# A prologue that takes its bound from the first parts of the keys, and more fill in the first turns: attention beside a long convolution on one Trainium2 core

## The chip, the core and the metric

The kernel runs on one core of one Trainium2 chip (trn2). The metric is the time of one execution on the device in microseconds (us); of several runs the median is taken. Besides the runs there is one profiled execution, whose trace is quoted here. Engines: PE multiplies matrices (PEld loads its weights), ACT applies functions, DVE and POOL work element by element, SP issues DMAs.

## The reference

Two independent parts, written side by side into the output: attention with 32 query heads of 16 columns and one shared key and value head over 2048 positions, and a gated long convolution of 512 channels.

```python
q = (x @ wq).reshape(B, S, 32, 16).transpose(0, 2, 1, 3)
k, v = x @ wk, x @ wv                                  # one head, 16 columns
p = softmax(einsum("bhqd,bkd->bhqk", q, k) * 16 ** -0.5)
a = einsum("bhqk,bkd->bhqd", p, v) -> (B, S, 512) @ wo
...
kv = short_conv(k2, shift_k) * v2                      # four taps
b = q2 * (irfft(rfft(kv, 2S) * rfft(ssm_k, 2S))[:S] + kv * ssm_D)
return concatenate([a, b], -1)                         # x: 1 x 2048 x 512
```

## The kernel before, in words

**The main loop.** Queries are cut into 32 stacks; a stack is four heads and 512 positions. For each stack there are 16 blocks of 128 keys in two halves, `a` = 0 and 1, which gives 1016 tiles on this path. A tile is eight products of PE (`keys`, L937: keys 32 x 49 rows against queries) into a two-bank tile `s`, one exponential of ACT over 128 x 1024 (`exp`, L949), and in a later turn the products of the exponentials with the values (`pv`, L973). There are two `s` tiles in PSUM (pool `ps`), so the scores of tile t wait for the exp of tile t - 2. Two further two-bank tiles (pool `pf`, `pair()`) serve everything else.

**Numbers in parts.** A float32 operand is written as a sum of two float16 parts, "first" (`hi`) and "second" or lower (`lo`), and a product is taken as first x first + lower weight x first + first x lower. A row of a stack holds 49 entries: first part of q (rows 0 to 15), its lower part (16 to 31), a bound of the scores (row 32), and the first part again (33 to 48). The bound keeps the exponentials in range; it is made from the largest |k| and from |q| (`first_bound`, `first_rows`; `bound` for the later stacks). The largest |k| comes from `k_max`.

**The prologue** (`prologue`, before tile 0). x comes in four chunks of 512 positions, each as two DMAs on SP's queue. A chunk is turned by PE (`x_turn`, L576), ACT writes the first part (L589) and DVE the lower (L592). Stack 0's queries are made from chunk 0 (L770, twelve products), cut (L683), sent to DRAM as parts (`q_send`), and read back as a stack (`stack`, L893). k and v are one product of 32 columns (`kv`, L601, 48 products over four chunks), copied by ACT (L611); its rows are spread over the partitions by a float32 product (`kv_rows`, L617), clipped (`k_cut`, L622) and combined (`k_rows`, L629) into the key tile `kst`, chunk by chunk of 512 keys; the first 256 keys go ahead. `v_turn` (L635, L638) turns v. Products on zeros (`warm`, L567) stand between.

**Behind the prologue.** `attend` walks over the tiles. Each turn emits the scores and exp of tile x + 2, the value products that its plan gives, and then "fill" from eight threads (the rest of the queries, the convolution, the output projection, a spill of turned chunks to DRAM). `_Fill.turn` decides how much: it keeps a running lateness of PE in ns (a turn is `SLOT` = 916, scores 220, a value product pair 430, a fill product 216) and lets fill in as long as it stays below `LATE` = 200. `yield WAIT, n` is a thread's request to be left alone for 2n turns. `rest_of_q` makes key chunks 2 and 3 in its first turns, then the bound of the first group, then the other queries. The order of instructions on each engine is exactly the order in which they are written (a manual schedule), and an engine that waits holds up all behind it.

Of the kernel before, what the change touches and what calls it, by code (L numbers as in the profile page):

```python
# [8 lines left out]
F32 = mybir.dt.float32  # L9
F32R = mybir.dt.float32r  # L10
BF16 = mybir.dt.bfloat16
# [8 lines left out]
P = 128  # L20
# [29 lines left out]
SLOT, SCORES, PV, UNIT, LATE = 916, 220, 430, 216, 200  # L50
# [59 lines left out]
class _Emit:  # L110
# [421 lines left out]
    def load(self):  # L532
# [6 lines left out]
        nc.scalar.dma_start(wkv[:, :, DH:32], I["A_wv"].rearrange("(k p) e -> p k e", p=P))  # L539
        self.msk = self.c.tile([P, 295], F32, name="msk")  # L540
        nc.scalar.dma_start(self.msk, I["msk"])
        xa = w.tile([P, 4, D], F32, tag="sp", bufs=1, name="xa")
# [12 lines left out]
        for g in range(1, 4):  # L555
            nc.sync.dma_start(wqf[g], wq[:, :, g * P : (g + 1) * P])
# [4 lines left out]
        self.parts(nc.gpsimd, self.wkv[:, 0], self.wkv[:, 1], wkv, WS)  # L561
        self.wqf = wqf
# [6 lines left out]
    def x_turn(self, c, b, between=lambda: None, cut=None):  # L569

        nc = self.nc

        def turn(dp, rows):
            for e in range(2):
                for i in rows:
                    nc.tensor.transpose(  # L576
                        b[dp][:, e, i * P : (i + 1) * P],
                        self.xin[c][i // 2][:, i % 2, (2 * dp + e) * P : (2 * dp + e + 1) * P],
                        self.ident,
                    )  # L580

        for rows in (range(2), range(2, 4)):
            for dp in range(2):
                turn(dp, rows)
            if rows.start == 0:
                between()
        for dp in range(2):
            hi, lo = (self.xT[c][:, i, 2 * dp : 2 * dp + 2, :] for i in range(2))
            nc.scalar.mul(hi, b[dp], XS)  # L589
            if cut is not None and dp == 0:  # L590
                self.q_hi(0, 0, cut)
            nc.vector.scalar_tensor_tensor(lo, b[dp], XS, hi, ALU.mult, ALU.subtract)  # L592
        if cut is not None:
            self.q_abs(0, 0, cut)

    def kv(self, b):

        order = [(i, j, dk) for dp in range(2) for i, j in ((0, 0), (1, 0), (0, 1)) for dk in (2 * dp, 2 * dp + 1)]
        for x in order:
            for c in range(4):  # L600
                self.nc.tensor.matmul(  # L601
                    b[32 * c : 32 * c + 32, :],
                    self.wkv[:, x[0], x[2], :],
# [27 lines left out]
    def v_turn(self, kv, b):  # L631

        nc = self.nc
        for t in range(4):
            nc.tensor.transpose(b[:, t * P : (t + 1) * P], kv[:, t * P : (t + 1) * P], self.ident)  # L635
# [831 lines left out]
```

## Time and profile before

| | us |
|---|---|
| runs, median of 3 | 1006.04 (1002.65 to 1006.18) |
| profiled execution | 1004.97 |
| its span, first to last instruction | 1003.1 |
| PE, ACT, DVE, POOL busy | 941.7, 951.4, 744.6, 172.7 |
| mean granted TensorE clock | 0.992 of full |

A row of a timeline has the start in us, the length, the engine, the line of the kernel, the operation, what it writes and reads, its shape and a count; in brackets the idle time before it and what ended that. Rows of groups have a count, then busy us and the mean in ns of one, then the idle time before them.

### The profile page before, as it was taken

The numbers are of one execution on the slowest core, as the hardware profiler recorded it, in microseconds if no ns is written. First come the engines' busy times: TensorE is split into PE (matmuls) and PEld (weight loads), VectorE is DVE, ScalarE is ACT, GpSimd is POOL, SyncE is SP. The second block draws the span as 40 slices with busy tenths as digits, with TensorE's granted clock in tenths as the row PEclk, the third lists the DMA queues.
The fourth block names the chain that finished last, engine by engine and source line by source line (L and its number), as shares of the span: only waits on it lengthen the run. The fifth ranks groups of instructions, "written<-read, shape, count | busy, mean of one in ns | idle before, by whom it ended". The sixth has DMA issues, their size and how long they took to land.

```text
span 1003.1 us, 51275 instructions
## 1 busy us (share of the span) xinstructions
PE 941.7 (94%) x23471; PEld 459.7 (46%) x23471; DVE 744.6 (74%) x963; ACT 951.4 (95%) x1033; POOL 172.7 (17%) x305
## 2 busy tenths in 40 slices
PE   7999999999999999999989999999889989989996
PEld 4344454444544444444544545444334444444453
DVE  4637966988528988989888688599998828667752
ACT  4699999999999999989999999999999999999994
POOL 2442211410004000100054353000000032111000
PEclk9799999999999999999999999999999999999999
DMA  6262442333213111222143344111111143121101
GB/s 228 82 191 77 134 125 86 106 91 91 71 55 99 62 44 45 87 85 65 44 141 120 95 148 125 43 42 37 54 44 44 48 124 109 55 71 43 49 10 47
DMA packets 69461, 83.12 MB, mean 83 GB/s; under 512 B 20816, under 2 KB 58550, under 8 KB 69238
## 3 DMA queue, kind: packets, MB, share of 16 engines
q1 hardware_dynamic: 47430, 43.78, 13.7%
q0 software_dynamic: 20320, 35.46, 12.1%
q8 instruction: 185, 3.03, 1.3%
q10 hardware_dynamic: 1488, 0.54, 0.2%
q14 instruction: 38, 0.31, 0.1%
HBM read 54.66 MB, written 25.03 MB: 79 GB/s over the span
## 4 chain that ended last, share of the span: by engine, by line
PE 51%; ACT 25%; DVE 14%; issue 6%; DMA 2%; SPq 0%; POOL 0%; ACTq 0%; DVEq 0%
ACT p L949 25%; PE f L973 24%; PE s L937 14%; PE f L250 11%; DVE own L1036 3%; DVE sp L169 1%; DVE ao L982 1%; DMA xb<-in_A_x 1%; DVE sp L290 1%; DVE ao L983 1%; DMA qd<-qp 1%; DVE sp L435 0%; PE f L617 0%; DVE own L1025 0%; DVE t L435 0%
## 5 line engine op out<-in xcount | busy, mean ns | idle before, releaser
L949 ACT ACTIVATE p<-s 128x1024 f32<-128x1024 f32 x1016 | 938.3, 1067 | 18.4 <-PE s L937 16.3
L973 PE MATMUL f<-p,vx 64*32 64x512 f32 (+1 forms) x8880 | 551.1, 555 | 1.8 <-DVE cut L683 1.1
L937 PE MATMUL s<-st,kst 49*32 49x512 f16 x8128 | 427.7, 382 | 33.3 <-ACT p L949 29.2
L937 PEld LDWEIGHTS <-kst 49*32 49x32 f16 x8192 | 199.8, 89 | 400.0 <-issue 353.8
L973 PEld LDWEIGHTS f<-p,vx 64*32 64x32 f32 x8880 | 175.8, 106 | 30.1 <-issue 4.6
L169 DVE TENSOR_TENSOR sp<-sp 128x1024 f32<-128x1024 f32 x96 | 111.1, 1215 | 0.0
L290 DVE COPY sp<-f 128x1024 f32<-128x1024 f32 x32 | 39.1, 1223 | 64.9 <-PE f L250 64.8
L295 POOL DMA_DIRECT2D ff<-in_ff x64 | 34.7, 546 | 277.1 <-ACT p L949 275.6
L982 DVE COPY ao<-f 128x512 f32<-128x512 f32 (+1 forms) x33 | 22.2, 674 | 56.7 <-PE f L973 56.6
L250 PE MATMUL f<-wo,o 64*32 64x512 f16 x1440 | 57.1, 375 | 1.7 <-DVE cut L683 0.9
L169 DVE TENSOR_TENSOR sp<-sp,sp 128x1024 f32<-128x1024 f32 x48 | 56.1, 1217 | 0.3
L250 PE MATMUL f<-xT,wq 64*32 64x512 f16 x1344 | 52.8, 375 | 1.7 <-DVE gm L733 1.2
L295 POOL DMA_DIRECT2D fi<-in_fi x32 | 17.8, 562 | 180.4 <-ACT p L949 180.4
L250 PE MATMUL f<-hT,ff 64*32 64x256 f32 x1024 | 40.8, 377 | 1.3 <-DVE sp L290 1.2
L250 PE MATMUL f<-a,ff 64*32 64x256 f32 x1024 | 41.2, 378 | 0.7 <-DVE a L407 0.6
L467 DVE TENSOR_TENSOR r<-f,q 128x512 f32<-128x512 f32 x16 | 11.0, 689 | 41.2 <-PE f L250 41.2
L250 PE MATMUL f<-sp,fi 64*32 64x256 f32 x1024 | 40.3, 376 | 0.9 <-DVE r L467 0.9
L469 POOL DMA_DIRECT2D out<-r x32 | 17.8, 562 | 124.6 <-DVE r L467 114.0
L405 DVE TENSOR_TENSOR a<-a,t 128x512 f32<-128x512 f32 x48 | 33.2, 692 | 1.6
L396 DVE TENSOR_TENSOR t<-kk,tpb 128x512 f32<-128x512 f32 (+1 forms) x50 | 33.0, 663 | 0.8 <-DMA qd<-qp 0.8
L323 POOL DMA_DIRECT2D hin<-in_B_ssm_k x32 | 21.1, 663 | 64.4 <-ACT p L949 63.0
L250 PEld LDWEIGHTS <-o 64*32 64x32 f16 x1440 | 22.8, 93 | 15.6 <-DVE wp L1156 1.5
(166 smaller groups left out, 731.1 us busy)
## 6 DMA issues: line engine op xcount, KB each, us to landing
ff<-in_ff POOLq DMA_DIRECT2D x64, 128.0 KB, 2.9
od<-ao SPq DMA_DIRECT2D x60, 128.0 KB
qd<-qp SPq DMA_DIRECT2D x48, 128.0 KB
st<-qd SPq DMA_DIRECT2D x62, 98.0 KB
kk<-in_B_k POOLq DMA_DIRECT2D x32, 128.0 KB, 2.9
v<-in_B_v POOLq DMA_DIRECT2D x32, 128.0 KB, 3.2
hin<-in_B_ssm_k POOLq DMA_DIRECT2D x32, 128.0 KB, 5.5
fi<-in_fi POOLq DMA_DIRECT2D x32, 128.0 KB, 3.0
```

The costliest lines, as they stand in the source:

```text
L169: v.tensor_tensor(part(out), part(a), part(b), op)
L250: y = self.nc.tensor.matmul(out[j : j + 32, cols], w[r, j : j + 32], x[r], start=half == m == 0, stop=half == 1 and m == k - 1,)
L290: self.nc.vector.tensor_copy(out, self.both.rearrange("p i (q n) -> p i q n", q=2))
L295: self.paced(self.nc.gpsimd.dma_start(t[:, i], self.I[n][:, 2 * m2 + i]))
L323: self.paced(nc.gpsimd.dma_start(dst, src))
L396: nc.vector.tensor_tensor(out[:, n], kk[:, x], tap(i, n.stop - n.start), ALU.mult)
L405: nc.vector.tensor_tensor(a, a, t, ALU.add)
L937: self.nc.tensor.matmul(s[j : j + 32, e, :], self.kst[rows, k * P + j : k * P + j + 32], self.st[n][rows, a, cols], start=True, stop=True,)
L949: self.exps[u % 4] = self.nc.scalar.activation(self.pt[u], s, AF.Exp, scale=LN2 * DH**-0.5 / SC / SC)
L973: nc.tensor.matmul(self.acc[e][32 * j : 32 * j + 32, m], vx[rows, :], y, start=k == 0, stop=stop)
L982: nc.vector.tensor_copy(a, self.acc[0][:, m])
L1036: v.scalar_tensor_tensor(g, g if i < 4 else y, c[i], y if i else x.bitcast(BF16), ALU.add, ALU.mult)
```

## The change

It has five parts.

1. The bound of stack 0 is made from a largest |k| that `kv_max` computes from first parts alone (16 products of 32 columns, all four chunks, in their own bank). The first 256 keys are computed apart (`kv_first`, 12 products of 16 columns). The full k and v follow in three groups (`kv(.., 0, 0)`, `(1, 0)`, `(0, 1)`); for chunk 3 the third group moves into `rest_of_q`, and so do the other keys of chunks 2 and 3, v of chunk 3, and a second run of `k_max` over the final k, which checks that the first bound was large enough.
2. Chunk 3 is turned right behind chunk 2, without the query products between; ACT saves its turned values to `xa` and its lower part is made later (`rest_of_q`). The products on zeros between the steps are gone, except the first ten.
3. Stack 0's queries go from the on-chip parts straight into the stack tile by twelve copies on SP (`first_stack`); the copies to DRAM and the loads of the other groups' query weights come behind them. POOL makes the first part of the queries; it also makes the parts of v's weights between the query's two parts, and their load goes to the end of SP's x loads.
4. One of the two rows of the bound is written by ACT instead of DVE. Stack 2 is loaded at the 22nd tile of stack 1 instead of the 6th.
5. `LATE` becomes 290 for the first 288 turns and stays 200 afterwards.

```diff
-SLOT, SCORES, PV, UNIT, LATE = 916, 220, 430, 216, 200
+SLOT, SCORES, PV, UNIT = 916, 220, 430, 216
+LATE, FULL = (290, 200), 288
...
+    def kv_max(self, b, c, dks):
+        for dk in dks:
+            for i in c:
+                self.nc.tensor.matmul(
+                    b[32 * i : 32 * i + 32], self.wkv[:, 0, dk, :], self.xT[i][:, 0, dk, :], start=dk == 0, stop=dk == 3
+                )
...
     def first_rows(self, b, st, a):
-        for e in range(2):
-            r = slice(BR + 64 * e, BR + 64 * e + 1)
-            self.nc.vector.tensor_scalar(st[r, a, :], b[r, e, :], f, -60000.0, ALU.mult, ALU.max)
+        r = [slice(BR + 64 * e, BR + 64 * e + 1) for e in range(2)]
+        self.nc.vector.tensor_scalar(st[r[0], a, :], b[r[0], a, :], f, None, ALU.mult)
+        self.nc.scalar.activation(st[r[1], a, :], b[r[1], a, :], AF.Copy, scale=f)
+    def first_stack(self, qp):
+        t = self.w.tile([P, 2, 512], F16, tag="st", bufs=2, name=self.nm("st"))
+        for a in range(2):
+            for i, rows in ((0, (0, BR + 1)), (1, (DH,))):
+                for r in rows:
+                    for e in range(2):
+                        h = DH * (e + 2 * a)
+                        self.nc.sync.dma_start(t[64 * e + r : 64 * e + r + DH, a, :], qp[h : h + DH, i, :])
...
+        cut = self.q_cut(q)
+        nc.gpsimd.tensor_scalar(qp[:, 0, :], cut, 1.0, None, ALU.mult)
+        self.kv_parts(slice(DH, 32))
+        nc.gpsimd.tensor_tensor(qp[:, 1, :], cut, qp[:, 0, :], ALU.subtract)
+        st = self.first_stack(qp)
...
+        nc.scalar.copy(self.xa[:, 2:4], t3[1])
+        nc.scalar.copy(self.xa[:, 0:2], t3[0])
+        self.kvb = kvb = self.pair()
+        self.kv(kvb[:, 0, :], 0, 0, four, four)
+        for a in both:
+            self.first_bound(b, a)
+        for a in both:
+            self.first_rows(b, st, a)
+        self.kv(kvb[:, 0, :], 1, 0, four, four)
+        self.exp(0, self.scores(0))
+        self.kv(kvb[:, 0, :], 0, 1, four, range(3))
+        self.exp(1, self.scores(1))
+        nc.vector.tensor_copy(self.kvt[0:96], kvb[0:96, 0, :])
+        self.kv_rows(self.kvt, 0, rows)
...
     def rest_of_q(self):
-        for c in range(2, 4):
-            yield 1, 2000, NEW, 1
-            b = self.bank()
-            self.kv_rows(self.kvt, c, b)
-            self.k_chunk(c, b)
-        yield from self.bounds((0,), 0)
+        yield WAIT, 3
+        for dp in range(2):
+            yield 0, 1300
+            self.x_lo(3, dp, self.xa[:, 2 * dp : 2 * dp + 2])
+        yield 1, 2000, NEW, 1
+        self.kv_rows(self.kvt, 2, kvb[:, 1, :])
+        self.k_chunk(2, kvb[:, 1, :])
...
+            self.kv(kvb[:, 0, :], 0, 1, range(n, n + g), (3,))
...
+        self.kv_rows(self.kvt, 3, kvb[:, 1, :])
+        self.k_chunk(3, kvb[:, 1, :])
+        yield 2, 1400, CONT, 2
+        self.bound((0,), 0, kvb[:, 1, :])
...
-            if t - self.base[n] == (6 if n else 22) and n + 1 < NQ:
+            if t - self.base[n] == (6 if n > 1 else 22) and n + 1 < NQ:
...
-        room = (LATE - self.late - max(0, SCORES + PV * more - SLOT)) // UNIT
+        room = (LATE[i >= FULL] - self.late - max(0, SCORES + PV * more - SLOT)) // UNIT
```

Three places show the new order. First ACT, from the turning of chunk 3 (`x`, `f` are PSUM tiles) to exp 0, before:

```order
L589 ACTIVATE xT<-f_228 128x1024
L672 CAST qp_247<-cut_226 128x512
L589 ACTIVATE xT<-x_229 128x1024
L678 ACTIVATE qa_253<-cut_226 128x512
L611 COPY kv<-x_272 128x512
L786 CAST kh_337<-kc_335 128x256
L638 ACTIVATE vx<-x_325 128x4x4x16
L949 ACTIVATE p_365<-s_356 128x1024
```

and the same stretch of ACT in the changed kernel:

```order
L582 ACTIVATE xT<-x_235 128x1024
L582 ACTIVATE xT<-f_236 128x1024
L809 COPY k_258<-x_257 16x256
L811 ACTIVATE qa_272<-cut_203 128x512
L822 CAST kh_301<-kc_299 128x256
L827 COPY xa<-f_236 128x1024
L828 COPY xa<-x_235 128x1024
L717 ACTIVATE st_211<-f_303 1x512 x2
L1026 ACTIVATE p_361<-s_352 128x1024
```

The cast of the queries and the work on v have left ACT; the two saves of chunk 3 and two rows of the bound (`st`) have come in, between the cast of the first keys and exp 0.

Second PE, from the scores of tile 1 to those of tile 2 (`s` with the two lowest numbers above tile 0's; LDWEIGHTS and the further products of a tile left out). Before:

```order
L937 MATMUL s_372<-st_267,kst 32x512
...
L937 MATMUL s_395<-st_267,kst 32x512
...
L617 MATMUL f_406<-kv,msk 128x512
```

In the changed kernel:

```order
L1014 MATMUL s_375<-st_211,kst 32x512
...
L632 MATMUL f_311<-kv,msk 128x512
L651 MATMUL f_303<-ident,kv 128x96 x4
L632 MATMUL f_311<-kv,msk 128x512
L1014 LDWEIGHTS kst
L1014 MATMUL s_415<-st_211,kst 32x512
```

Two row projections and the turn of v now stand between the second and the third tile of scores.

Third PE again, at tiles 14 and 15 of the changed kernel, where the keys of chunk 3 are spread (`kv`, `f_311` is the bank that they share with the bound):

```order
L1014 MATMUL s_641<-st_211,kst 32x512
L632 MATMUL f_311<-kv,msk 128x512
L697 LDWEIGHTS wb
L697 MATMUL f_311<-qa_272,wb 32x512
L1014 LDWEIGHTS kst
L1014 MATMUL s_665<-st_211,kst 32x512
```

Before, the projection of chunk 3 stood ahead of tile 5 and the bound of the first group by itself at tile 10:

```order
L617 MATMUL f_443<-kv,msk 128x512
...
L937 MATMUL s_451<-st_267,kst 32x512
...
L709 MATMUL f_563<-qa_253,wb 32x512
...
L937 MATMUL s_570<-st_267,kst 32x512
```

Projection and bound have come together, in one bank, with no scores between them.

259 lines of the change are left out of this document (146 added, 113 removed).

## The prediction

> **What bounds the kernel now.** I read the page first: engine shares, chain, costliest groups.
>
> ```profile
> span 1003.1 us, 51275 instructions
> PE 941.7 (94%) x23471; PEld 459.7 (46%) x23471; DVE 744.6 (74%) x963; ACT 951.4 (95%) x1033; POOL 172.7 (17%) x305
> L949 ACT ACTIVATE p<-s 128x1024 f32<-128x1024 f32 x1016 | 938.3, 1067 | 18.4 <-PE s L937 16.3
> ```
>
> ACT's 1016 exponentials (exps) fill the span, 938.3 of 1003.1 us. The end is where ACT's last exp puts it, so an edit counts only by how much earlier ACT is in its row of exps once that row runs undisturbed. Second view: the timeline of ACT alone.
>
> ```profile
> 32.15 1.02 ACT L949 ACTIVATE p<-s 128x1024 f32<-128x1024 f32 x1
> 34.32 3.97 ACT L949 ACTIVATE p<-s 128x1024 f32<-128x1024 f32 x4 [1.15 <-PE s L937]
> 39.56 1.02 ACT L949 ACTIVATE p<-s 128x1024 f32<-128x1024 f32 x1 [1.27 <-PE s L937]
> 41.76 15.41 ACT L949 ACTIVATE p<-s 128x1024 f32<-128x1024 f32 x16 [1.17 <-PE s L937]
> 57.52 59.15 ACT L949 ACTIVATE p<-s 128x1024 f32<-128x1024 f32 x64 [0.35 <-ACT p L949]
> ...
> 308.96 70.08 ACT L949 ACTIVATE p<-s 128x1024 f32<-128x1024 f32 x76 [0.47 <-PE s L937]
> ...
> 642.67 125.72 ACT L949 ACTIVATE p<-s 128x1024 f32<-128x1024 f32 x137 [0.23 <-PE s L937]
> ```
>
> Undisturbed, an exp takes 125.72/137 = 0.917 us. Exps are counted from 0: exp 0 starts at 32.15, exp 6 at 41.76, exp 22 at 57.52. Without gaps exp 22 would start at 32.15 + 22 x 0.917 = 52.3, so 5.2 us are lost between the first exp and this one; the three long gaps wait for PE (s L937). Third view: windows, for the granted clock (the last columns are clock, DMA share, GB/s).
>
> ```profile
> 16.00:18.00 2.00, 2.00 (x14) 1.16 (x13) 0.89 (x2) 1.78 (x2) 0.00 (x0) 1.00 1.02 245
> 24.00:26.00 2.00, 1.45 (x15) 0.28 (x7) 1.19 (x3) 0.32 (x1) 1.92 (x2) 1.00 0.46 139
> 26.00:28.00 2.00, 1.69 (x6) 0.63 (x6) 0.53 (x1) 0.26 (x1) 1.83 (x3) 1.00 0.24 77
> 28.00:28.50 0.50, 0.20 (x1) 0.00 (x0) 0.18 (x2) 0.40 (x1) 0.50 (x1) 0.90 0.24 78
> 31.50:32.00 0.50, 0.50 (x11) 0.13 (x10) 0.00 (x0) 0.28 (x1) 0.50 (x1) 0.69 0.00 0
> 35.00:35.50 0.50, 0.50 (x2) 0.00 (x0) 0.50 (x2) 0.50 (x2) 0.42 (x2) 0.72 0.00 0
> 42.00:42.50 0.50, 0.50 (x32) 0.27 (x16) 0.00 (x0) 0.50 (x1) 0.00 (x0) 0.95 0.00 0
> ```
>
> The first two columns after the times are the stretch and PE's busy time. The clock is halved from about 28.4 to 31.7 and from 35.2 to 42.0; the steps lie 3.4 us or a multiple apart. Just there, PE does what the first exps wait for.
>
> **The change, part by part.** These durations carry the sum.
>
> ```profile
> L592 DVE SCALAR_TENSOR_TENSOR xT<-x,xT 128x1024 f16<-128x1024 f32 x4 | 4.8, 1222 | 9.0 <-ACT xT L589 9.0
> L589 ACT ACTIVATE xT<-x 128x1024 f16<-128x1024 f32 x4 | 4.0, 1023 | 4.9 <-PE x L576 4.9
> L273 POOL TENSOR_SCALAR wq<-wqf 128x512 f16<-128x512 f32 x2 | 3.0, 1490 | 0.2
> L770 PE MATMUL x<-xT,wq 128*128 128x512 f16 x12 | 2.8, 379 | 0.0
> L673 POOL TENSOR_TENSOR qp<-cut,qp 128x512 f16<-128x512 f32 x1 | 1.2, 1165 | 11.4 <-ACT qp L672 11.4
> L729 DVE TENSOR_SCALAR st<-f 1x512 f16<-1x512 f32 x2 | 1.4, 690 | 0.3 <-PE f L722 0.3
> L610 DVE TENSOR_REDUCE km<-x 128x1 f32<-128x512 f32 x1 | 0.7, 692 | 0.7 <-PE x L601 0.7
> L683 DVE TENSOR_SCALAR cut<-x 128x512 f32<-128x512 f32 x1 | 0.7, 681 | 0.0
> L622 DVE TENSOR_SCALAR kc<-f,msk 128x256 f32<-128x256 f32 x1 | 0.5, 544 | 1.6 <-PE f L617 1.6
> L273 POOL TENSOR_SCALAR wkv<-wkvf 128x128 f16<-128x128 f32 x1 | 0.5, 540 | 7.3 <-DMA wkvf<-in_A_wv 7.3
> L786 ACT CAST kh<-kc 128x256 f16<-128x256 f32 x1 | 0.4, 404 | 1.8 <-DVE kc L622 1.8
> L646 PE MATMUL x<-kx,msk 128*128 128x4 f32 x2 | 0.4, 262 | 0.0
> L651 DVE TENSOR_SCALAR wb<-msk,kmr 128x8 bf16<-128x8 f32 x1 | 0.2, 231 | 0.1
> ```
>
> And from the timelines of PE and SP:
>
> ```profile
> 15.58 0.60 PE L576 MATMUL x<-ident,xc 128*128 128x128 f32 x4
> 22.89 2.02 PE L601 MATMUL x<-xT,wkv 128*32 128x512 f16 x29 [0.21 <-DVE xT L592]
> 26.07 2.05 SPq L893 DMA_DIRECT2D st<-qd  x4
> 32.30 1.12 PE L617 MATMUL f<-kv,msk 32*128 32x512 f32 x2
> 36.86 2.07 PE L617 MATMUL f<-kv,msk 32*128 32x512 f32 x2
> 42.16 0.39 PE L937 MATMUL s<-st,kst 49*32 49x512 f16 x8
> 42.38 1.05 PE L973 MATMUL f<-p,vx 64*32 64x512 f32 x16
> 43.24 0.41 PE L937 MATMUL s<-st,kst 49*32 49x512 f16 x8
> ```
>
> *Queries.* Their twelve products no longer wait for all of chunk 2's transposes. The last four stand behind chunk 2's second half, which landed before 15.58; what PE has ahead of it ends at 13.6 by the same durations, so the wait ends between 13.6 and 15.6; I take 14.3. Less is loaded ahead of it than now: in the row 16:18 the DMA engines are still full with the other groups' weights, which come later in the new order. Four transposes (0.44 to the next four, 0.60 to the last end), four products (2.8/12 = 0.23 each) and DVE's cut (0.68) end at 16.6. POOL then casts (1.49), splits v's weights (three operations on half a tile, 0.8 to 1.5 in all, from the 0.54 of the whole; I take 0.8) and subtracts (1.17): 20.1. SP issues eight more of the twelve copies at 2.05/4 = 0.51: 24.2. Landing is not shown for them; the four copies issued from 26.07 to 28.1 were in place before exp 0 at 32.15, so 0 to 4 us; I take 2: 26.2. The scores that need them come later than that, so this path hides, and the 3 q copies and the weights of the other groups behind them on SP hide as well.
>
> *Keys.* Chunk 3 is turned when the query cut and the second half of chunk 1's lower part have freed its banks: 16.6 + 1.22 = 17.8, transposes 0.9, ACT's last part 18.95 to 19.97. Now the last products wait for that chunk's lower part until 22.89. The first 256 keys (twelve products of half width, 1.4) follow when DVE has made chunk 2's first lower part and freed their bank, at 19.0: 20.4. The maximum takes the first parts only: 0.9 for three chunks side by side and 0.9 for chunk 3 alone: 22.2. Then DVE 0.69 and 0.54, the small step 0.23, PE 0.39, DVE 0.16 and 0.23: the weights of the bound at 24.8, key rows at 25.3. ACT casts (0.40) until 24.05 and only then saves chunk 3 (1.02 each): 25.1 and 26.1. PE's bank for k and v waits for the first of these. So the added saves set the next step, not the bound.
>
> *To exp 0.* From 25.1: sixteen products (2.02/29 = 0.07 each, 1.1), four bounds (0.45), sixteen products beside the two rows on DVE and ACT (0.69 each), scores, 0.5 to the exp: 27.9 with the full clock; with half the clock from 25.0 (one step of 3.4 ahead of 28.4) to 28.4, where the first three of these take twice as long, it is 29.5. PE has only about 1.0 us of work between 22.2 and 25.1, against 1.45 and 1.69 of 2 us in the rows that precede the fall at 28.4. So I take the half clock: exp 0 at 29.5, 2.65 earlier than 32.15.
>
> *To exp 2.* Now the order costs. Between the second and the third score PE has two row projections and a turn of v, and they wait for a copy on DVE. Scores 1 and exp 1 at 30.6; k and v's last products end at 30.1, the copy is done at 31.0 (taken as the cut's 0.68 for the same columns), projection 1.12, DVE's cut 0.54 of the bank, projection 1.12: 33.9, exp 2 at 34.4. Before it was 34.32 + 1.0 = 35.3. Of 2.65 us there is **0.9 left**.
>
> *To exp 22.* Scores take 0.22 (42.16 to 42.38) and a pair of value products 0.86 (42.38 to 43.24). The projections of chunks 2 and 3 stand at tiles 8 and 14, the second with the bound behind it in the same bank: PE waits there for DVE's cut of 512 columns (0.54 for 256, so 0.54 to 1.1; I take 0.8), so 1.1 + 0.1 + 0.8 + 0.2 in one turn. Laid out tile by tile this leaves ACT without work for 0.7 at exp 9 and 1.4 at exp 15, and 0.3 in between. Before, 1.27 and 1.17 went at exps 5 and 6, with the slow clock: a projection took 2.07 instead of 1.12. With these gaps and 0.94 to 0.96 for the exps in between, exp 22 starts at 55.9 instead of 57.52: **1.6 us gained**.
>
> *Fill.* The planner's limit rises from 200 to 290 for the first 288 turns. Per pair of tiles two fill products of 216 fitted; now the sequence is 3, 2, 2. The order says what comes of it: 231 products are placed by tile 50 before and 175 now, 1343 and 1365 by tile 288. It makes up for what starts later, no more. From exp 22 to exp 291 ACT took 308.96 - 57.52 = 251.4 us for 269 exps, 4.8 more than 269 x 0.917. If the fuller turns double that loss or remove it, that is +4.8 or -4.8; nothing in the rows favours a sign, and I take 0, with ±3 as the usual part of it. The other stacks' loads and the spill move by turns with 8 us and more of reserve: 0.
>
> **Sum.** 1004.97 of the profiled execution (span 1003.1) less 1.6 is 1003.4. That execution lies 1.1 below the median of the three runs, 1006.04, and inside them (1002.65 to 1006.18). I say 1003.5.
>
> The Trainium skill, "TensorE: Matmul & The Clock Gate", section "Part 1: The HAM clock gate (the "warmup" mystery)", says the clock is halved after a window of about 3.4 us without work and is full after a busy one. The 3.4 us agrees with the steps above; the cause doesn't, since the clock fell at 28.4 with PE busy 1.69 of the 2 us before. By that rule no window of the new prologue is idle throughout and the clock stays full, which is the first rival.
>
> **Rivals.**
> - *Full clock throughout* (chance 0.2). Nothing is taken off, exp 0 is at 27.9 and all that follows moves with it: 1.6 more, 1001.8. Against it: both falls of before came with more work on PE than now.
> - *The slow clock returns until 42* (0.17), as it did from 35.2 on. Then the second parts, the projections (2.07) and the first value products take twice as long: exp 0 at 30.2, k and v's last products end at 31.6, copy, projection, cut, turn and projection put exp 2 at 38.6; exp 6 comes at 42.9, and with 16 exps at 0.96 and the gaps of 2.2 exp 22 at 60.5, a **loss of 3.0 us: 1008.0**. It decides once the half clock lasts over 35.1: until there it costs 1.4 of the 1.6, beyond that the balance is a loss.
> - *Queries late* (0.05). If v's weights land late, POOL holds back the lower part of the queries and SP all copies behind it. It costs nothing until the copies land after 28.9, then us for us; at 2 us a copy in turn it would be some 4 us, 1007.5.
> - *The fill decides* (0.13): stalls between turns come or go by 5 us, 998.5 or 1008.3, as likely one as the other.
>
> **How the numbers follow.** The forecast itself, exp 0 early and most of it given back, has 0.45. The range takes in the full clock with some of the fill's gain and the slow clock: 999 to 1008.5. What a measurement of this kernel can tell from no change is about 0.5%, 5 us. Faster by more needs the full clock and a kind fill: 0.18. Slower by more needs the slow clock and an unkind one: 0.1. Within: 0.72.
>
> **What would show it.** Exp 0 at 29 to 30 and exp 2 at 34 to 35 in ACT's timeline; a wait of ACT of over 1 us near exp 15, with PE waiting for DVE's cut at the bound behind the projection of chunk 3; the copies of chunk 3 just ahead of the first products of k and v; the clock at 0.5 for one window from about 25. Wrong is my sum if exp 22 doesn't lie between 54 and 58; if it lies there and the time is off by more than 3 us, the fill was mis-sized.

## The result, and the profile after

The changed kernel takes 1023.26 us (median of 6 runs, 1022.54 to 1024.56) where the kernel before takes 1006.11 (6 runs beside it, 1002.65 to 1007.12): a ratio of 1.017, 95% interval 1.0159 to 1.019. It is 1.7% slower; the prediction was 1003.5 with a range up to 1008.5. The profiled execution has a span of 1022.4 us against 1003.1. Of all the executions told of below, one, of the version on POOL with exps 2 and 3 put forward, took 1557 us at a mean granted clock of 0.556 of full; its ratio is taken without it.

The page of the changed kernel, its span, its engines and the group of exps (busy us and mean ns, then the idle time before them and what ended it):

```profile
span 1022.4 us, 51338 instructions
PE 945.5 (92%) x23493; PEld 462.5 (45%) x23493; DVE 747.8 (73%) x971; ACT 955.6 (93%) x1035; POOL 174.6 (17%) x308
L1026 ACT ACTIVATE p<-s 128x1024 f32<-128x1024 f32 x1016 | 940.5, 1064 | 38.6 <-PE s L1014 36.5
```

No engine has much more to do: the exps take 940.5 us where they took 938.3. What grew is ACT's idle time before them, from 18.4 to 38.6 us: 20.2 of it, against 19.3 more in the span. Scores of PE end 36.5 of it (16.3 before). So something makes PE late more often. ACT's timeline shows where (start, length, count; in brackets the idle time before the row):

```profile
29.70 1.02 ACT L1026 ACTIVATE p<-s 128x1024 f32<-128x1024 f32 x1 [0.82 <-PE s L1014]
31.01 1.02 ACT L1026 ACTIVATE p<-s 128x1024 f32<-128x1024 f32 x1 [0.28 <-PE s L1014]
34.75 3.77 ACT L1026 ACTIVATE p<-s 128x1024 f32<-128x1024 f32 x4 [2.72 <-PE s L1014]
39.62 2.94 ACT L1026 ACTIVATE p<-s 128x1024 f32<-128x1024 f32 x3 [1.10 <-PE s L1014]
43.37 6.01 ACT L1026 ACTIVATE p<-s 128x1024 f32<-128x1024 f32 x6 [0.80 <-PE s L1014]
51.09 2.10 ACT L1026 ACTIVATE p<-s 128x1024 f32<-128x1024 f32 x2 [1.72 <-PE s L1014]
53.58 5.77 ACT L1026 ACTIVATE p<-s 128x1024 f32<-128x1024 f32 x6 [0.39 <-PE s L1014]
59.69 50.73 ACT L1026 ACTIVATE p<-s 128x1024 f32<-128x1024 f32 x54 [0.34 <-ACT p L1026]
113.42 1.02 ACT L1026 ACTIVATE p<-s 128x1024 f32<-128x1024 f32 x1 [3.00 <-PE s L1014]
...
991.41 16.61 ACT L1026 ACTIVATE p<-s 128x1024 f32<-128x1024 f32 x18 [0.20 <-PE s L1014]
```

The exps are counted through these rows: exps 0 and 1 alone, then 4, 3, 6, 2 and 6, so exp 22 is the last of the row at 53.58 and starts at about 58.3. Exp 0 is 2.4 us earlier than before, exp 2 0.5 us earlier, and exp 22 already 0.8 us later. Counted in the same way to exp 291 and to the last, number 1015:

| us | exp 22 starts | exps 22 to 291 | exps 291 to 1015 | last exp starts |
|---|---|---|---|---|
| before | 57.5 | 251.4 | 678.7 | 987.7 |
| changed | 58.3 | 264.0 | 684.7 | 1006.9 |
| difference | +0.8 | +12.5 | +6.0 | +19.3 |

So the loss doesn't lie in the prologue, where nearly all the edits are, but behind it. It comes in few pieces: waits of ACT of 0.5 us and more for the scores of an exp add up, behind exp 22, to 26.6 us in the changed kernel (18 waits) and to 9.8 before (10). The largest ones up to exp 500 follow, each with the row of PE that stood in front of it. The first is the wait at 113.42, in the timeline of all engines:

```profile
107.31 0.39 PE L697 MATMUL f<-qa,wb 128*32 128x512 bf16 x2
108.80 0.41 PE L1014 MATMUL s<-st,kst 49*32 49x512 f16 x8
109.60 0.69 DVE L409 TENSOR_TENSOR a<-a,v 128x512 f32<-128x512 f32 x1 [2.44 <-DMA v<-in_B_v]
110.21 0.68 DVE L699 TENSOR_SCALAR gn<-f 40x512 f16<-40x512 f32 x1
110.81 0.67 DVE L733 TENSOR_REDUCE gm<-f 48x1 f32<-48x512 f32 x1
111.58 1.31 PE L252 MATMUL f<-a,ff 64*32 64x256 f32 x16 [2.37 <-issue]
112.41 0.91 PE L1014 MATMUL s<-st,kst 49*32 49x512 f16 x8
```

PE made the products of a bound at 107.31 and the scores at 108.80; the next it has to do are products of the convolution (`f<-a,ff`). DVE waited 2.44 us for a load of v, made the operand `a`, and only then took the bound out of its bank (`gn`, `gm`). PE goes on 0.1 us after the last of these, and the scores stand behind in its queue. (For this wait of PE the profile itself names nothing, "issue"; that it is for `gm` is read from the times.) Nothing in the queue is wrong; PE simply comes too soon to it. The others, in PE's timeline:

```profile
137.63 0.67 PE L252 MATMUL f<-a,ff 64*32 64x256 f32 x16 [2.07 <-DVE a L409]
207.88 0.84 PE L252 MATMUL f<-xT,wq 64*32 64x512 f16 x24 [1.97 <-DVE gm L733]
306.92 0.61 PE L1050 MATMUL f<-p,vx 64*32 64x512 f32 x1 [1.80 <-issue]
447.30 1.96 PE L1050 MATMUL f<-p,vx 64*32 64x512 f32 x16 [2.27 <-DVE sp L292]
```

Most have the same form. In front of 12 of the 18 waits (17.3 us of the 26.6) stands a product of the fill, or a value product, whose operand or bank DVE hasn't finished with by the profile. In front of three (3.00 us at 113.42, 2.65 at 308.28, 0.97 at 430.51) PE waits for something that the profile doesn't name.

The last three (0.88 us at 115.33, 0.79 at 140.43, 1.01 at 453.12) have no wait of PE in front of them. They lie where PE itself is slow: at some of its waits the granted clock falls to half. Windows of the changed kernel (behind the comma stands PE's busy time, the clock is third from the end):

```profile
108.00:111.40 3.40, 1.21 (x32) 0.28 (x16) 1.80 (x3) 2.42 (x3) 0.00 (x0) 1.00 0.27 85
111.40:114.90 3.50, 3.32 (x49) 2.04 (x54) 3.50 (x7) 1.02 (x1) 0.00 (x0) 0.51 0.04 9
138.60:142.20 3.60, 3.60 (x64) 1.90 (x56) 3.46 (x7) 2.54 (x3) 0.00 (x0) 0.53 0.40 134
445.80:452.80 7.00, 5.50 (x72) 2.36 (x80) 6.86 (x13) 2.66 (x3) 0.00 (x0) 0.51 0.30 88
```

The scores at 112.41 take 0.91 us, those at 108.80 took 0.41. Between exps 22 and 1015 these stretches make 13.7 us of half clock; before there is one of 3.4, at 431. An estimate from these numbers: 10.2 us more at half the clock cost PE at most 5.1 us of work, while this part is 18.5 us longer. What the slow clock costs ACT by itself no run shows.

### The profile page after: what moved, and what is told of

It reads as the page before. It is cut to its first block, busy times and chain, and to the rows that moved or that the text cites. A ratio compares the mean times of both kernels' runs of the same rounds, so it can differ in the third digit from the quotient of the medians.

```text
span 1022.4 us, 51338 instructions
## 1 busy us (share of the span) xinstructions
PE 945.5 (92%) x23493; PEld 462.5 (45%) x23493; DVE 747.8 (73%) x971; ACT 955.6 (93%) x1035; POOL 174.6 (17%) x308
## 3 DMA queue, kind: packets, MB, share of 16 engines
q8 instruction: 185, 3.03, 1.3%
## 4 chain that ended last, share of the span: by engine, by line
PE 51%; ACT 29%; DVE 11%; issue 7%; DMA 1%; POOL 0%; ACTq 0%; SPq 0%; DVEq 0%
ACT p L1026 29%; PE f L1050 24%; PE s L1014 14%; PE f L252 10%; DVE own L1113 3%; DVE ao L1059 1%; DVE ao L1060 1%; PE f L614 1%; DVE sp L292 1%; PE f L570 0%; DMA v<-in_B_v 0%; DVE x L1110 0%; PE f L577 0%; DVE sp L222 0%; DVE own L1102 0%
## 5 line engine op out<-in xcount | busy, mean ns | idle before, releaser
L1026 ACT ACTIVATE p<-s 128x1024 f32<-128x1024 f32 x1016 | 940.5, 1064 | 38.6 <-PE s L1014 36.5
L1014 PEld LDWEIGHTS <-kst 49*32 49x32 f16 x8192 | 197.5, 90 | 396.5 <-issue 350.4
L292 DVE COPY sp<-f 128x1024 f32<-128x1024 f32 x32 | 39.1, 1223 | 56.1 <-PE f L252 55.9
L297 POOL DMA_DIRECT2D fi<-in_fi x32 | 17.3, 546 | 172.6 <-ACT p L1026 172.6
L471 POOL DMA_DIRECT2D out<-r x32 | 17.3, 546 | 119.9 <-DVE r L469 119.7
L407 DVE TENSOR_TENSOR a<-a,t 128x512 f32<-128x512 f32 x48 | 33.1, 690 | 1.6
L252 PEld LDWEIGHTS <-wq 64*32 64x32 f16 x1344 | 21.5, 93 | 19.0 <-DVE gm L733 5.3
```

The lines of the kernel that those rows point to most:

```text
L252: y = self.nc.tensor.matmul(out[j : j + 32, cols], w[r, j : j + 32], x[r], start=half == m == 0, stop=half == 1 and m == k - 1,)
L292: self.nc.vector.tensor_copy(out, self.both.rearrange("p i (q n) -> p i q n", q=2))
L297: self.paced(self.nc.gpsimd.dma_start(t[:, i], self.I[n][:, 2 * m2 + i]))
L407: nc.vector.tensor_tensor(a, a, t, ALU.add)
L1014: self.nc.tensor.matmul(s[j : j + 32, e, :], self.kst[rows, k * P + j : k * P + j + 32], self.st[n][rows, a, cols], start=True, stop=True,)
L1026: self.exps[u % 4] = self.nc.scalar.activation(self.pt[u], s, AF.Exp, scale=LN2 * DH**-0.5 / SC / SC)
```

## The experiments

Each run stands beside runs of the kernel before on the same chip; the ratio has its 95% interval. One term is used below. The *fill order* is which fill product stands in which turn. The planner makes it from its constants and from the requests of the threads, and it can be read off the program without running it. There are two of them here, which I call the first (near that of before) and the second (that of the changed kernel). The turns in which the products of the queries and the convolution stand (a turn has the number of the tile whose scores it makes):

| turns of | before | first order | second order |
|---|---|---|---|
| queries of chunk 0, group 1 | 12 to 22 | 16 to 24 (18 to 26 with the new prologue) | 22 to 30 |
| other queries of chunk 0 | 30 to 52 | 34 to 52 | 38 to 60 |
| first products of the convolution | from 54 | from 54 | from 62 |
| queries of chunk 1 | 92 to 178 | 92 to 168 | 134 to 190 |
| queries of chunk 2 | 212 to 312 | 182 to 228 | 262 to 322 |
| queries of chunk 3 | 342 to 418 | 298 to 370 | 354 to 498 |

In the second order the turns from 62 to 131 hold nothing but the convolution (and one bound); in the first its products stand between those of the queries from turn 92 on.

### Fuller turns, or a late start?

Four runs, with the old prologue unless said. The first has the new limit alone:

```diff
-SLOT, SCORES, PV, UNIT, LATE = 916, 220, 430, 216, 200
+SLOT, SCORES, PV, UNIT = 916, 220, 430, 216
+LATE, FULL = (290, 200), 288
```

> The kernel before with the planner's limit of 290 in the first 288 turns and nothing else. Two theories of the 17 us. Theory F (fuller turns): with 290 PE has no room left to take up a wait of a fill product for DVE, and that costs the 12 us that the changed kernel lost between exp 22 and exp 291; it expects 1016 to 1020 us here, with exp 22 to exp 291 in 260 to 264 us instead of 251.4. Theory S (shift): the fill is only dealt anew because it starts some 8 turns later; it expects 1002 to 1010 here and no more idle ACT in the first 291 exps than in later ones.

The second has the rest of the queries eight turns later and stack 2 at the 22nd tile, with the old limit:

```diff
     def rest_of_q(self):
+        yield WAIT, 4
...
-            if t - self.base[n] == (6 if n else 22) and n + 1 < NQ:
+            if t - self.base[n] == (6 if n > 1 else 22) and n + 1 < NQ:
```

> The kernel before, limit 200, with the thread of the remaining queries starting 8 turns later and stack 2 loaded at the 22nd tile, which that needs. Theory F expects 1003 to 1009 us, as before, since no turn is fuller. Theory S expects 1012 to 1022, since the order of the fill moves as in the changed kernel.

The third has both, and this makes the first order:

> The kernel before with both, the later start and the limit of 290 for 288 turns, but the old prologue. Theory F expects 1016 to 1020 us; theory S 1012 to 1022, near the run with the later start alone; a theory that only the prologue's own steps cost (its exps up to 22 are 0.9 us later than before) expects 1003 to 1009.

The fourth is the changed kernel with `LATE, FULL = (301, 200), 288`:

> The changed kernel with 301 in place of 290. Theory F expects a little more of the same, 1022 to 1028 us. Theory S expects that 11 ns in the planner's limit deal the fill anew, and a time at least 4 us away from 1023 in either direction, more likely below.

Measured (the kernel before at 1005.41): the limit alone 1006.93 (ratio 1.0019, 0.9999 to 1.0039), the late start alone 1004.96 (1.0002, 0.9988 to 1.0017), both 1007.28 (1.0019, 1.0003 to 1.0034), the changed kernel with 301 1025.42 (1.0195, 1.0162 to 1.0228). By the medians neither fuller turns nor the late start, nor both, costs more than 2 us, and a still higher limit doesn't help. So theory F fails with the limit alone (1016 to 1020 was said), theory S with the late start alone (1012 to 1022) and with 301 (at least 4 us from 1023); read off the program, 301 deals 27 turns anew, none behind turn 282. With both, the waits of ACT of 0.5 us and more add up to 10.1 us behind exp 22, not to 26.6.

### Prologue and fill order, exchanged

What remains is the new prologue itself, or its fill order. Both can be exchanged. The old prologue takes the second order when its threads are held back a little further, with the limit of 290 and stack 2 as above:

```diff
     def rest_of_q(self):
+        yield WAIT, 4
...
         yield from self.bounds((0,), 0)
+        yield WAIT, 4
```

From turn 22 on each turn holds the same fill products as in the changed kernel.

> The old prologue with the changed kernel's fill: the rest of the queries begins eight turns later and keeps off for eight more behind the bound of the first group, stack 2 is loaded at the 22nd tile, 290 for the first 288 turns; from turn 22 on each turn holds the same fill products as in the changed kernel. Theory D (the cost lies in which fill product stands in which turn, whatever the prologue does): 1018 to 1025 us, and ACT waits for scores for over 30 us. Theory P (the cost comes with the new prologue: its later steps, its late loads of v and of the other weights on SP's and POOL's queues): 1003 to 1010, and some 16 to 20 us of such waits. In between (1010 to 1018) both have a part.

And the changed kernel takes the first order when one request is made four turns shorter:

```diff
     def rest_of_q(self):
-        yield WAIT, 3
+        yield WAIT, 1
```

> The changed kernel with the rest of the queries begun four turns earlier, and nothing else; from turn 28 on each turn holds the fill products that the old prologue has with 8 turns of delay and 290 (1007.3 us). Theory D (which product stands in which turn): 1004 to 1010 us, waits of ACT for scores 16 to 22 us, and exp 22 within 1 us of the changed kernel's. Theory P (the prologue): 1018 to 1025, waits over 30 us.

Measured (the kernel before at 1005.02):

| | first order | second order |
|---|---|---|
| old prologue | 1007.28 (ratio 1.0019) | 1024.41 (ratio 1.016, 1.0124 to 1.0195) |
| new prologue | 1011.07 (ratio 1.0059, 1.0037 to 1.0082) | 1023.26 (ratio 1.0174) |
| exp 22 to exp 1015, old / new prologue | 930.5 / 929.3 | 949.0 / 948.6 |

The last row settles it: the stretch behind exp 22 takes 930 us with one order and 949 with the other, whichever prologue stands before it. The group of exps on the page of the old prologue with the second order, and then of the new one with the first:

```profile
L952 ACT ACTIVATE p<-s 128x1024 f32<-128x1024 f32 x1016 | 940.7, 1064 | 35.6 <-PE s L940 33.5
```

```profile
L1026 ACT ACTIVATE p<-s 128x1024 f32<-128x1024 f32 x1016 | 939.5, 1065 | 24.4 <-PE s L1014 22.4
```

And the waits are the same, one by one. ACT's timeline of the old prologue with the second order, at the places quoted above:

```profile
114.49 1.02 ACT L952 ACTIVATE p<-s 128x1024 f32<-128x1024 f32 x1 [4.00 <-PE s L940]
139.21 1.02 ACT L952 ACTIVATE p<-s 128x1024 f32<-128x1024 f32 x1 [1.65 <-PE s L940]
```

with PE waiting at 112.85 for the convolution's operand, at 208.20 (1.97 us) for `gm` and at 447.13 (2.27 us) for `sp`, within 1.3 us of the places of the changed kernel. So the prologue has no part in the loss behind exp 22. The slow clock goes with the order as well: in that stretch it is halved for 13.7 us in both traces of the second order, and not at all in these two of the first.

The order costs more than this slow clock does. One of the four runs of the old prologue with the second order had a mean granted clock of 0.992 and took 1016.59 us, the others 0.984 to 0.988 and 1024.10 to 1024.85; with the first order it was 0.990 to 0.996 and 1007.28 in the median. So some 9 us of the loss stay where the clock is hardly slower; since this is a single run, the figure is an estimate.

For the new prologue with the first order theory D had said 1004 to 1010 and exp 22 within 1 us of 58.3. Both were missed, ahead of exp 22.

### What the new prologue is worth without this loss

With the first order the changed kernel is still 6 us slower than before, and this loss lies ahead of exp 22, which starts at 63.7. ACT's and PE's rows of that run:

```profile
43.24 1.02 ACT L1026 ACTIVATE p<-s 128x1024 f32<-128x1024 f32 x1 [5.32 <-PE s L1014]
```

```profile
36.70 2.07 PE L632 MATMUL f<-kv,msk 32*128 32x512 f32 x2
41.60 1.01 PE L614 MATMUL f<-xT,wkv 128*32 128x512 f16 x2 [2.84 <-DVE kc L637]
```

and DVE's:

```profile
37.63 3.20 DVE L586 SCALAR_TENSOR_TENSOR xT<-xa,xT 128x1024 f16<-128x1024 f32 x2
40.75 0.80 DVE L637 TENSOR_SCALAR kc<-f,msk 128x512 f32<-128x512 f32 x1
```

The projection of chunk 2 comes 5 us sooner (36.70; 41.77 in the changed kernel), and DVE has the lower part of chunk 3 (3.20 us) ahead of the cut of these keys (`kc`), for which PE waits. The clock has a part too: it is halved here from 35.6 to 45.8, and the projection of 1.12 us takes 2.07. Two runs, one with each order, tried to take the early exps from behind such work. Scores and exps of tiles 2 and 3 stand right behind exp 1, and the first bound gets the other bank of its pair (the turn of v the one it leaves):

```diff
         self.exp(1, self.scores(1))
+        for t in (2, 3):
+            self.exp(t, self.scores(t))
...
-        self.bound((0,), 0, kvb[:, 1, :])
-        self.bound_max((0,), 0, kvb[:, 1, :])
+        self.bound((0,), 0, kvb[:, 0, :])
+        self.bound_max((0,), 0, kvb[:, 0, :])
```

> As the run before, and besides the second and third pair of scores and exps stand right behind exp 1, ahead of the projections, and the bound of the first group has its bank apart from v's, so that PE doesn't wait there for DVE's cut of chunk 3. ACT should start exp 22 some 2 to 2.5 us earlier than in the changed kernel, at 56. By theory D the time is 1002 to 1008, the best chance to beat the kernel before (1005.4 in the last runs); by theory P 1016 to 1023.

> The changed kernel with its own fill, and the two moves of the run before (two more scores and exps ahead of the projections, the bound's bank apart). Exp 22 some 2 to 2.5 us earlier, at 56. If what ACT loses behind exp 22 is independent of it, the time is 2 to 2.5 us below the changed kernel: 1020 to 1022. Theory P, if the loss hangs on when the prologue ends: 1010 to 1018.

Both missed. With the first order 1011.26 (ratio 1.0051, 1.0032 to 1.007), exp 22 at 65.9; with the second 1024.77 (1.0205, 1.0177 to 1.0233), exp 22 at 58.2. Exp 2 did come at 32.0 instead of 34.8 with the second order, but by exp 22 nothing of it was left. PE's row at the bound in that run shows why the bank didn't help:

```profile
50.17 0.38 PE L697 MATMUL f<-qa,wb 128*32 128x512 bf16 x1 [1.55 <-DVE kc L637]
```

It still waits for the cut of the keys, which reads the pair's other bank; and that cut begins at 49.31, 0.7 us after its projection has ended, since DVE has the output weights to prepare first. ACT waits 2.29 us at exp 15 there.

Next the lower part of chunk 3 goes to POOL, which waits for weights at that time, on top of the shorter request:

```diff
-        nc.scalar.copy(self.xa[:, 2:4], t3[1])
-        nc.scalar.copy(self.xa[:, 0:2], t3[0])
+        for dp in (1, 0):
+            nc.scalar.mul(self.xa[:, 2 * dp : 2 * dp + 2], t3[dp], XS)
+        for dp in both:
+            y, z = (self.xT[3][:, i, 2 * dp : 2 * dp + 2, :] for i in range(2))
+            nc.gpsimd.tensor_tensor(z, self.xa[:, 2 * dp : 2 * dp + 2], y, ALU.subtract)
...
-            self.x_lo(3, dp, self.xa[:, 2 * dp : 2 * dp + 2])
```

> The run with the rest of the queries begun four turns earlier (1011.1 us) and besides the lower part of chunk 3 made by POOL out of the saved chunk, right behind the key rows, where POOL waits for the weights; each turn holds the same fill products as there. The theory of its loss: DVE made that lower part (3.3 us, at half the clock) ahead of the cut of chunk 2's and 3's keys, and PE stood behind it with the scores of exp 5 (a wait of 5.3 us of ACT). Then that wait falls to about 1 us, exp 22 starts at 57 to 59 instead of 63.6, the 929.4 us from exp 22 to the last exp stay within 2 us, and the time is 1004 to 1007. The rival, that the early scores wait for something else (the clock, the keys' copies): exp 22 stays over 61.5 and the time over 1008.

then besides with the bound two turns behind the keys and the start two turns earlier:

```diff
-        yield WAIT, 1
         for dp in range(2):
...
+        yield WAIT, 1, CONT
         yield 2, 1400, CONT, 2
         self.bound((0,), 0, kvb[:, 1, :])
```

> As the run before; besides, the rest of the queries begins two turns earlier still and the bound of the first group keeps off for two turns behind the keys of chunk 3, so that PE need not wait in that turn for DVE's cut; from turn 28 on each turn holds the same fill products. The wait of 1.7 us of ACT near exp 15 goes, exp 22 starts at 55.5 to 57, and the time is 1002.5 to 1005.5: at best 2 to 3 us below the kernel before. If ACT's early lead is taken back by later waits, the 929 us behind exp 22 grow by what was gained and the time is 1004 to 1007.

and with exps 2 and 3 put forward as above:

> As the run before, and the scores and exps of tiles 2 and 3 stand right behind exp 1, ahead of the projections; the fill is the same. Exp 2 at 32 instead of 34.8, exp 22 up to 1.5 us earlier than in the run before (54.5 to 56), the time 1001.5 to 1004.5. If what PE owes comes due anyway, exp 22 and the time don't move by more than 0.5 us, as when the same two moves were made with the changed kernel's fill (58.2 against 58.3).

Measured (the kernel before at 1006.07): 1007.94 (ratio 1.0023, 1.0005 to 1.0041), 1007.25 (1.0019, 1.0 to 1.0038) and 1009.06 (1.0031, 1.001 to 1.0052). The 930 us behind exp 22 hold in all (930.2, 927.1, 927.1). With the lower part on POOL exp 22 starts 2.2 us earlier than in the run with the first order alone, and the wait at exp 5 falls from 5.32 to 3.03 us. But exp 22 starts at 61.6, 62.6 and 63.0, so the expected 55 to 59 was missed each time. In the second run the wait for the bound is gone, and another has come near its place: PE stands 1.42 us behind DVE's `ks`, ACT 1.38 at exp 15. PE's and ACT's rows of that run:

```profile
35.19 2.07 PE L632 MATMUL f<-kv,msk 32*128 32x512 f32 x2
38.23 1.44 PE L614 MATMUL f<-xT,wkv 128*32 128x512 f16 x3 [0.97 <-DVE kc L637]
```

```profile
34.91 1.94 ACT L1028 ACTIVATE p<-s 128x1024 f32<-128x1024 f32 x2 [3.67 <-PE s L1016]
40.30 2.12 ACT L1028 ACTIVATE p<-s 128x1024 f32<-128x1024 f32 x2 [3.46 <-PE s L1016]
```

A projection of 1.12 us takes 2.07: by the windows the clock is at half from 32.7 to 42.9, and again from 53.2 to 56.6.

### Is it the clock?

Fourteen products on zeros fill PE's gaps of the prologue, once in the changed kernel, once in the version with POOL and the bound apart. `b` is the pair of the bounds:

```diff
         self.kv_max(kb[:, 1, :], (3,), range(4))
+        b = self.pair()
+        self.warm(b[:, 1, :], zero, 4)
...
-        b = self.pair()
+        self.warm(b[:, 1, :], zero, 4)
         self.k_max(b[:, 0, 0:4], km, kmr)
+        self.warm(b[:, 1, :], zero, 4)
...
         self.exp(1, self.scores(1))
+        self.warm(b[:, 1, :], zero, 2)
```

> The changed kernel with fourteen products on zeros put back into PE's gaps between 21 and 30.5 us (four each behind the maximum, the row projection and the small product of the bound, two behind the second score); the fill is the same. Theory: the prediction's miss of 2.4 us at exp 22 (58.3 against 55.9) is the slow clock, which lasted from 24 or 25.7 to 29 and came back from 36.2 to 39.7; with PE busy in its gaps at least one of the two windows stays full, exp 0 starts at 28 to 29 and exp 22 at 55.5 to 57, and the time is 1020 to 1022.5. Rival: the products take PE's time at half clock and the windows fall all the same: exp 22 at 58 to 59.5, time 1022 to 1025.

> The same fourteen products in the version with the lower part on POOL, the bound apart and the other deal (1007.3 us; there the clock was halved from 25.8 to 29.2 and from 32.6 to 42.6). Theory: with fuller windows exp 22 comes at 56 to 59 instead of 62.5 and, with 927.3 us from there to the last exp, the time is 1001 to 1004: below the kernel before. Rival: the windows fall all the same, exp 22 stays at 62 to 63.5 and the time at 1007 to 1009.

Measured (the kernel before at 1004.68): 1024.88 (ratio 1.0179, 1.0138 to 1.022) and 1008.24 (1.0034, 1.0015 to 1.0054), with exp 22 at 59.2 and 62.4, as the rivals had said. Windows of the changed kernel, read as above:

```profile
22.00:23.00 1.00, 0.63 (x2) 0.22 (x2) 0.33 (x1) 0.00 (x0) 0.00 (x0) 0.83 0.12 30
23.00:24.00 1.00, 0.51 (x2) 0.52 (x3) 0.35 (x2) 0.75 (x2) 0.00 (x0) 0.50 0.11 27
29.00:29.50 0.50, 0.50 (x10) 0.12 (x8) 0.00 (x0) 0.00 (x0) 0.00 (x0) 0.52 0.70 163
36.00:36.50 0.50, 0.23 (x8) 0.00 (x0) 0.50 (x1) 0.50 (x1) 0.50 (x1) 0.81 0.00 0
39.50:40.00 0.50, 0.50 (x24) 0.22 (x13) 0.50 (x1) 0.38 (x1) 0.50 (x1) 0.78 0.83 281
```

and with the products on zeros in it:

```profile
25.00:26.00 1.00, 1.00 (x18) 0.44 (x20) 0.00 (x0) 0.77 (x1) 0.00 (x0) 1.00 0.12 30
29.60:33.00 3.40, 3.17 (x18) 1.04 (x26) 1.97 (x5) 1.02 (x1) 0.49 (x1) 1.00 0.90 251
33.00:33.50 0.50, 0.50 (x17) 0.22 (x17) 0.45 (x1) 0.03 (x1) 0.50 (x1) 0.65 0.79 225
39.50:40.00 0.50, 0.50 (x9) 0.00 (x0) 0.00 (x0) 0.37 (x1) 0.42 (x1) 0.53 0.00 0
50.00:50.50 0.50, 0.20 (x1) 0.00 (x0) 0.47 (x2) 0.00 (x0) 0.00 (x0) 0.71 0.00 0
```

A mean between 0.5 and 1 tells when the clock changed: 0.83 from 22 to 23 is two thirds of it at full speed. So the changed kernel has half the clock from 22.7 to 29.5 and from 36.3 to 39.7. With the zeros the first stretch is gone, and exp 0 starts at 28.5 instead of 29.7, exp 2 at 33.5 instead of 34.8. The second one begins sooner and is twice as long, 33.1 to 40.0, and a third follows from 50.2 to 53.6, where the wait at exp 15 grew from 1.72 to 2.73 us. Exp 22 starts at 59.2, later than 58.3. So the zeros moved the slow clock and took none of it away: up to exp 22 it lasts 10.2 us in both kernels. In the version on POOL they did take away the first stretch (25.9 to 29.3), and exp 22 came 0.2 us earlier.

Two other traces show the changed prologue with a first stretch of 3.4 us instead of 6.8: those of the limit 301 and of the loads without a tie to an exp (the next run). There exp 22 starts at 57.9 and 57.4. By these single executions, 3.4 us of slow clock there are worth 0.2 to 0.9 us at exp 22, much less than the miss of 2.4. What the second stretch costs isn't known: no trace of the changed kernel is without it.

### Loads ahead of their time

One run asked how much of the waits in the second order is due to the loads. In the changed kernel the convolution's loads lose their tie to an exp (`paced`), so that POOL issues them when their buffers are free; each instruction stands where it stood.

```diff
-            self.paced(self.nc.gpsimd.dma_start(t[:, i], self.I[n][:, 2 * m2 + i]))
+            self.nc.gpsimd.dma_start(t[:, i], self.I[n][:, 2 * m2 + i])
...
-                self.paced(nc.gpsimd.dma_start(v[:, i], self.vr[:, 2 * m2 + i, cs]))
+                nc.gpsimd.dma_start(v[:, i], self.vr[:, 2 * m2 + i, cs])
```

(and in the same way for the key rows.)

> The changed kernel, with the convolution's loads (its key rows, its v rows, its tables) issued by POOL as soon as their buffers are free, instead of each behind an exp; every instruction stands where it stood. Theory: in the changed kernel's turns the convolution's products run so close behind the elementwise work and the loads that PE stands for DVE and DVE for v. With the loads ahead the waits of DVE for v (6.5 us in all) go, and with them the two waits of ACT at 113 to 115 (3.9 us) and part of those at 138 to 140 (2.5 us): 1017 to 1020.5. The waits behind other work of DVE (209, 308, 356, 449) stay. If buffers, not pacing, hold the loads, nothing moves: 1022 to 1025.

Measured: 1022.46 (1019.61 to 1023.64; ratio 1.0177, 1.0147 to 1.0208). The expected 1017 to 1020.5 holds only for the profiled execution, the fastest of the four (1019.61). There the waits at 113 and 115 are gone, and exps 22 to 1015 take 945.4 us instead of 948.6; the other waits of over 1 us are all there, two of them in PE's timeline:

```profile
132.68 0.67 PE L252 MATMUL f<-a,ff 64*32 64x256 f32 x16 [2.03 <-DVE a L409]
201.35 0.84 PE L252 MATMUL f<-xT,wq 64*32 64x512 f16 x24 [1.97 <-DVE gm L733]
```

So in that execution the tied loads were the cause of the one wait and of no other of over 1 us. In the medians 0.8 us are left of it, which the runs can't tell from nothing: the loads are not the main thing.

## Why the prediction was wrong

**The step that failed is the fill.** The prediction counted it: 231 products against 175 by tile 50, 1343 against 1365 by tile 288, "It makes up for what starts later, no more", and took "0, with ±3 as the usual part of it" and 4.8 us at the extremes. The exchanged runs give this term its size: 12 us between exps 22 and 291 and 6 to 7 behind them, with the old prologue (263.8 and 685.3 against 251.4 and 678.7 before) as with the new one (264.0 and 684.7 against 251.4 and 677.9 with the first order). Two things were wrong in it. It compared how many products were placed, not which stood in which turn; the waits come from the latter. And it ended at exp 291, while the two orders differ up to turn 498 and beyond. Its bound came from doubling the loss that the kernel before has there, as if an order could only repeat the waits of another one. The trace of before had the price of one such wait (PE behind DVE's `cut` or `sp`, 0.7 to 1.8 us of ACT each), and the order of the changed kernel could be read; the two were not put together. The change raises the limit and delays the queries, by its own request and by the work on chunk 3; neither the limit nor a delay of eight turns does harm alone, nor do both together, and four turns less of delay bring the other order back.

**Exp 0 and exp 2 were right**: 29.70 (said 29.5) and 34.75 (34.4). The order of the steps was as told: the copies of chunk 3 at 23.56 and 24.46 set the first products of k and v; exp 2 waits 2.72 us for the two projections behind DVE's copy. One part of it came out by luck: the clock fell at 22.7, not 25.0, and stayed at half until 29.5, while the steps ahead of it came about a microsecond earlier than said. (The terms of the way to the bound's weights add up to 24.4, not to the 24.8 written there; the forecast doesn't go by them, since the saves of chunk 3 come last.)

**Exp 22 was mis-sized**: 58.3 instead of 55.9, just outside the 54 to 58 that the prediction set itself, a loss of 0.8 us instead of a gain of 1.6. The gaps told for exps 9 and 15 are there (0.80 and 1.72, said 0.7 and 1.4), but also 1.10 us at exp 6 and 0.39 at exp 17, against 0.3 counted for the rest. The four are 1.6 us more than the sum had; exp 2 was 0.35 late, and the rest is in the exps themselves, 0.98 us each instead of 0.95. The wait at exp 6 lies in the second slow window, 36.3 to 39.7, that the forecast left to a rival. The gap at exp 15 was put down to the shared bank; the wait is for the cut that was named (0.97 us of PE), but another bank of the same pair didn't remove it.

**The queries hide**, as told: the last copy was issued by 25.8 (24.2 was said) and the scores that need them come at 29.0.

**The rivals.** The full clock and late queries didn't happen. The slow clock came back for one window, not two; the wait of 1.10 us at exp 6 lies in it, but what it cost in all no run shows (3.0 was said for two). "The fill decides" was the right rival, with 0.13, and its price of 1008.3 was too small by 15 us.

**What stays open.** The exchange shows that the order costs the 18 us, not which trait of it does. The 70 turns of the convolution alone hold 6.4 of the 26.6 us of waits; the others are spread up to exp 975, and their share of slow clock isn't separated.

No version with the new prologue beats the kernel before: the best, with the first order, the lower part on POOL and the bound apart, stands at 1.0019 (1.0 to 1.0038). Between 30 and 60 us each engine of it waits for another in turn (PE at half the clock, DVE's cuts, the banks of one pair), and the five runs that moved exp 2 forward by 1.3 us and more left exp 22 within 0.4 us of where it was, or later. Which of these sets exp 22 isn't settled.

## What to carry to other kernels

When a planner deals out work by a running count, a small change of its constants or of one thread's delay can deal a wholly different order: compare which work stands in which turn, and next to what, rather than how much. On an engine that works in order, work dealt in "spare" time is free only if its operands and banks are ready at that moment; one that isn't holds up the critical products behind it, here 0.5 to 4 us of ACT each time. Where a change touches both the code and the deal, exchange the two in runs of their own before anything is said of the code.

## What the runs showed of the hardware

- The clock was halved behind busy stretches too: with the products on zeros PE was busy, by the profile, for 3.17 of the 3.40 us from 29.6 to 33.0, and the clock fell at 33.1. The Trainium skill, "TensorE: Matmul & The Clock Gate", section "Part 1: The HAM clock gate (the "warmup" mystery)", ties the fall to a window without work; here the measurement says otherwise, and only the length agrees (36.3 to 39.7 is 3.4 us, 22.7 to 29.5 twice that). The start also varied, from 22.7 to 25.9, between kernels with nearly the same prologue, so a sum that hangs on one window is uncertain by 3.4 us of half clock.
- In the main loop of the changed kernel each fall stood behind a stretch with much waiting: PE was busy for 1.21, 1.33 and 1.84 of the 3.4 us ahead of 111.4, 138.7 and 445.9. But 1.44 of 3.4 us ahead of 207.9 and 1.62 ahead of 306.9 brought no fall.
- The lower part of a chunk took DVE 1.22 us in the prologue, where one operand comes out of PSUM (the memory that PE writes to); so it did with POOL at work all or nearly all through it (at 8.80 before, at 17.84 in the changed kernel). Out of the saved chunk, with both operands in the on-chip memory SBUF and POOL at work, it took 1.62 and 1.65 us (the two at 37.28 in the changed kernel), but also 1.21 and 2.18 (the two at 35.26 with the products on zeros). On POOL the same part took 4.21 for two (as one subtraction each, from values that ACT had scaled). What makes the difference was not tested by a run of its own.
